# Another order of the same steps: gate logits of the first two spans loaded first, W2 behind the first keys, W1 last of the weights

## The chip, the cores and the metric

The kernel runs on one core of a Trainium2 chip. The metric is the device time in microseconds (us) from start to end of one execution. The kernel before takes 141.34 us, the median of three runs (141.2 to 141.57).

## What is computed

A gated linear recurrence (32 independent sequences of 768 steps, head dimension 48) gives a matrix of 3072 tokens x 384, and that goes through a maxout layer:

```
f = 1 / (1 + exp(-f_logit))
for t in range(768):
    state = f[t][:, None] * state + outer(k[t], v[t])      # 48 x 48 per batch (4) and head (8)
    y[t] = q[t] @ state
x = y of all heads side by side                            # 3072 x 384
out = maximum(x @ w1, x @ w2) @ w_out                      # w1, w2: 384 x 1024, w_out: 1024 x 384
```

All inputs and the output are float32 in HBM; the kernel casts to bf16 for TensorE.

## The kernel before, in words

The tokens are cut into 12 spans of 256: span s has batch s % 4 and window s // 4, so spans 0 to 3 start with an empty state and every later span continues the one four before it. Each span goes through two parts.

- Recurrence, in two halves of 64 token pairs. Loads `Lf`, `Lk`, `Lq`, `Lv` (line 122, 384 KB each) bring the gate logits, keys, queries and values of a span into one of 27 slots of SBUF; the number behind the @ is the slot, and a load into a used slot waits until its last reader is done. On ScalarE (ACT), `E`, `F` and `G` make exp and log of the gate (lines 211, 215, 219). `e` (222) adds the logs of a token pair, the matmuls of `C` (226, 229) sum them up along time, and `X` and `Z` (236, 241) take the exponentials of the sums. `i`, `j`, `K`, `Q` (245, 249, 256, 259) scale the keys and queries, and `V` (a copy, 111) casts the values. TensorE (PE) transposes keys (`t`) and queries (`u`; lines 272 for spans 0 and 1, 279 for the others), `U` copies the transposes to SBUF, `A` (302) makes the scores, `m` (308) masks them, `S` and `y` (323) multiply state and values into the output of the span, `D` (366) makes the addition to the state, and `n`, `N` (383 to 388) bring the state up to date. `z` is a tiny copy that keeps `y` behind the first half of `S`.
- Maxout. Since max(a, b) = b + relu(a - b), the kernel uses wd = w1 - w2 and m2 = w2 @ w_out. `Y` (111) copies the transposed span out of PSUM, `d` (405) multiplies it with wd, `r` (414 on ACT, 416 on VectorE, DVE) is the relu, `o` and `p` (427) multiply with w_out and add x @ m2, `b` (111) copies the result out of PSUM, and `O` (440) stores it.
- The weights are prepared once, in the opening. `Wb0` to `Wb2` (138, 512 KB each) load the rows of W2, which `wc` casts, `wt` (449) transposes and `wx` copies; `Wo0` to `Wo3` (142, 384 KB each) load W_out, and `wo` casts it; `wm0` to `wm3` (464) sum up m2, one quarter for each quarter of W_out, and `wn` copies it out; `Wa0` to `Wa3` (135, 384 KB each) load W1, and `ws` (473) makes wd. They land in slots 0 to 11; the cast and the transposed W2 lie in slots 12 to 15.

The order of everything is written out by hand in one string, `ORDER`: one word for each step, with the span or part, the engine (a ScalarE, v VectorE, p GpSimd (POOL), s SyncE (SP)) and, after the @, a PSUM bank or a slot. `U1.1a@5` is half 1 of `U` of span 1, on ScalarE, from bank 5. A step stands on its engine's queue in the order of its words, and each engine works its queue strictly in that order; across engines only data and buffers (PSUM banks, slots, SBUF buffers) make one wait for another. All loads and stores are on SP's one queue: a load that waits for its slot, or a store that waits for its result, holds up every DMA behind it. The loop that turns words into instructions is

```python
    for word in ORDER.split():
        key, of, e, b = re.fullmatch(r"([A-Za-z]+)([0-9.]+)([avps]?)@?([0-9]*)", word).groups()
        steps[key](*map(int, of.split(".")), e, int(b or 0))
```

Of the kernel before, what the change touches and what calls it, by code (L numbers as in the profile page):

```python
# [17 lines left out]


ORDER = """  # L20
Wb2s Lf1s@8 Lf0s@2 Lq0s@22 g7p Lk1s@24 g6p g4p g2p Wb1s wc2a g5p g0p g3v wt2@5 Lq1s@25 E1 wx2v@5 F1 Lk0s@1
E0 e1p F0 C1@3 Lv1s@20 j0v G1 e0v Z1 C0@7 G0 Wb0s i1v X1 Lv0s@23 Z0 K1v wc1a Q0v t1@1 wt1@3 Wo1s j1v
U1.0a@1 Lf3s@16 Q1v u0@6 X0 Wa3s wx1a@3 i0v u1@5 Wo3s Wo2s U1.1a@5 V1v Wa2s K0v D1@2 Wo0s U0.1a@6 A1.1@0
A1.0@4 Lf2s@20 n1.0 n1.1 t0@7 wc0a m1.0@4 Wa0s V0p wt0@6 U0.0a@7 m1.1@0 D0@4 wo1p S1.0@2 wx0a@6 n0.0
A0.0@0 z1v@2 S0.0@6 n0.1 m0.0@0 z0a@6 A0.1@5 N0.1p y1 g1p m0.1@5 Wa1s E3 Lq3s@13 S1.1@2 S0.1@6 Y1.0a@2 y0
ws3v F3 Lk2s@21 Y0.0v@6 Y1.1a@3 wo3p d1.3@1 wm1@2 wo2a wm3@2 ws2v Lk3s@17 N1.1v d1.2@0 e3v wm2@2 wo0v
r1.1v@0 wm0@2 Lq2s@3 E2 Y0.1v@7 C3@7 F2 d0.3@5 ws0v wn2a@4 wn0a@2 e2v d1.0@0 Lf4s@23 X3 ws1v G3 C2@2
d0.0@6 Z3 wn1v@3 Lf5s@9 X2 d1.1@1 j3v G2 d0.1@7 Q3v r1.0a@0 Lv3s@19 d0.2@4 i2v r0.0a@6 o1.0@0 K2v r0.1a@4
Lv2s@10 i3v Z2 o0.1@7 K3v Lk4s@1 j2v Q2v t2@3 b0.1.0a@7 t3@1 u3@1 b1.0.0a@0 u2@3 E4 U3.2v@1 o0.0@5 U2.0a@3
Lq4s@23 U2.1v@4 Lq5s@24 E5 A3.0@6 Lf7s@17 A3.1@3 F4 V3p m3.0@6 o1.1@0 F5 e4p m3.1@3 G4 V2p b0.0.0a@5 D3@1  # L30
b1.1.0a@0 A2.0@6 e5p n3.0 D2@4 Lk5s@10 m2.0@6 S3.0@0 Lf6s@19 C4@3 z3a@0 i4p S3.1@0 y3 X4 n2.0 Z4 n3.1
S2.0@3 Lv4s@9 Y3.2a@0 A2.1@2 z2v@3 n2.1 S2.1@3 C5@6 m2.1@2 G5 d3.0@0 Z5 Lq9s@26 d3.3@7 X5 j4v j5v y2 Q4p
Lq6s@25 d3.2@6 Y2.2v@3 d3.1@1 r3.1a@6 Lf8s@11 i5v d2.0@5 K4p r3.0v@0 E7 d2.2@3 O0.2s E6 d2.3@4 d2.1@6 F7
K5v Lk6s@12 o3.1@7 F6 Q5p r2.0v@5 r2.1a@3 Lv5s@15 t4@0 V4v t5@4 e6p u5@4 u4@0 U5.2v@4 o2.0@2 U4.2a@0
Lq7s@20 e7p N2.1v j6v Lk7s@3 C6@6 G6 b2.0.0v@2 A4.1@3 E8 D4@0 Lv7s@22 o3.0@2 n4.0 b3.1.0a@7 N3.1v N4.0p
m4.1@3 Z6 X6 Q6p G7 n4.1 S4.0@6 b3.0.0a@2 A5.0@3 A4.0@0 F8 o2.1@2 m4.0@0 Lv6s@25 z4a@6 e8p V5a Lq8s@19
m5.0@3 i6p C7@5 b2.1.0a@2 y4 Z7 K6v X7 S4.1@6 A5.1@2 D5@0 Y4.2a@6 i7p m5.1@2 u6@4 Lf9s@12 t6@4 Lk8s@24
d4.0@6 U6.2a@4 n5.0 O1.2s d4.1@7 N5.0p K7p C8@0 r4.0v@6 d4.2@2 Lv10s@2 G8 d4.3@3 X8 n5.1 Z8 S5.0@6 N4.1p
r4.1a@2 A6.0@4 Lf11s@17 A6.1@0 z5v@6 V6p y5 m6.0@4 N5.1p S5.1@6 D6@2 Lf10s@21 Y5.2a@6 j7v o4.1@4 m6.1@0
V7a Lk10s@15 E9 n6.0 d5.2@0 N6.0p Lk9s@16 F9 b4.1.0v@4 d5.3@1 j9v d5.1@5 j8v r5.1a@0 d5.0@4 Q8p O3.2s  # L40
S6.0@6 r5.0a@4 D7@1 z6v@6 y6 Lq10s@22 Q7v G9 S6.1@6 E11 o4.0@4 e9p n7.0 Y6.2v@6 Lk11s@18 E10 i8v d6.3@7
N7.0v b4.0.0a@4 O2.2s n7.1 F10 d6.2@6 K8v Lv8s@19 d6.1@4 F11 n6.1 e10v C9@0 r6.1a@6 d6.0@3 Lv11s@3 i9p
o5.0@1 r6.0v@3 N7.1p G11 X9 Z9 K9p O4.2s t7@6 t8@2 Lv9s@17 u7@6 u8@2 U7.2a@6 C10@0 o5.1@5 j10v N6.1p
U8.2v@2 e11p b5.0.0a@1 G10 A7.0@6 i11v A7.1@2 b5.1.0a@5 i10p m7.0@6 C11@1 Z10 o6.0@4 O5.2s Z11 Lq11s@0
V10p X10 m7.1@2 X11 K10p V8a S7.0@0 A8.1@6 b6.0.0a@4 A8.0@2 z7v@0 y7 m8.1@6 Q9p S7.1@0 D8@4 o6.1@5 n8.0
Y7.2v@0 V9a V11a m8.0@2 d7.1@1 b6.1.0v@5 d7.0@0 N8.0v O6.2s K11v u9@6 r7.0a@0 t9@6 d7.2@4 U9.2v@6 d7.3@5
S8.0@0 r7.1a@4 D9@3 D10@6 z8v@0 D11@2 n9.0 y8 n10.0 N9.0p S8.1@0 N10.0v A9.1@3 Q10v A9.0@6 Y8.2a@0 o7.0@5
j11v n11.0 Q11p m9.0@6 o7.1@0 b7.0.0a@5 m9.1@3 N11.0p t10@3 b7.1.0v@0 t11@5 u10@3 u11@5 O7.2s U10.2v@3
d8.0@0 U11.1a@6 d8.1@1 U11.0a@5 d8.3@3 d8.2@2 r8.0a@0 S9.0@6 r8.1v@2 A11.1@4 A10.1@0 z9a@6 y9 m10.1@0
S9.1@6 o8.0@3 Y9.2a@6 m11.1@4 A11.0@6 b8.0.0v@3 A10.0@4 S11.0@0 m11.0@6 o8.1@3 m10.0@4 d9.3@7 b8.1.0a@3  # L50
z11v@0 d9.2@6 O8.2s d9.0@2 r9.1a@6 d9.1@3 S10.0@6 r9.0v@2 S11.1@0 y11 z10a@6 y10 Y11.0v@0 S10.1@6 Y11.1v@1
o9.1@5 Y10.2a@6 o9.0@4 b9.1.0v@5 d11.2@1 b9.0.0a@4 d10.0@2 O9.2s r11.4v@1 d10.1@3 d10.2@5 r10.0a@2 d10.3@6
d11.1@3 r10.1a@5 d11.3@2 r11.3v@3 o10.0@7 d11.0@3 b10.0.0v@7 o10.1@0 r11.2v@3 r11.5v@2 o11.0@5 b10.1.0a@0
O10.2s p11.1.1@2 b11.0.0v@5 O11.0s p11.1.0@1 b11.1.2a@2 O11.1.2s b11.1.1a@1 O11.1.1s
"""


# [479 lines left out]
```

## Time and profile before

| quantity | value |
|---|---|
| median of three runs | 141.34 us |
| the profiled execution, its own time | 140.85 us |
| its span, first to last instruction | 138.8 us |
| outside the span | 2.05 us |
| PE busy | 123.0 us (89%) |
| DVE / ACT / POOL busy | 102.6 / 85.0 / 48.7 us |
| moved by DMA | 28.68 MB, mean 207 GB/s |
| share of PE in the chain that ended last | 81% |

The profile is of one execution. Its page gives busy times of each engine, a strip of 40 equal slices of the span (here 3.47 us each), and the chain of work that ended last. The other views are the timeline (instructions in order of time; in brackets the idle time of the engine before one and what ended it), the chain in order of time, and the windows (busy time of each engine in chosen stretches; PEclk is the granted TensorE clock as a share of full speed). PE overlaps one matmul with the next, so two rows of PE can overlap in time, and the steady spacing of a step is shorter than its row.

### The profile page before, as it was taken

How to read it: one execution, taken by the hardware profiler on the slowest of the kernel's cores; microseconds unless marked ns; L12 is line 12 of the kernel's file. 1: busy time of each engine (PE TensorE's matmuls, PEld its weight loads, DVE VectorE, ACT ScalarE, POOL GpSimd, SP SyncE). 2: the span in 40 equal slices, each digit the busy share in tenths (PEclk: the TensorE clock that was granted, in tenths of full speed). 3: DMA queues.
4: the chain of work that ended last, by engine and by line, in shares of the span. 5: the costliest groups of instructions: out<-in, count | busy, mean ns of one | idle time of the engine just before them, and what ended most of it. 6: DMA issues, size and time to landing. Idle time of an engine off the chain costs nothing.

```text
span 138.8 us, 5704 instructions
## 1 busy us (share of the span) xinstructions
PE 123.0 (89%) x2543; PEld 93.7 (68%) x2543; DVE 102.6 (74%) x158; ACT 85.0 (61%) x129; POOL 48.7 (35%) x58
## 2 busy tenths in 40 slices
PE   0225689999999999899899999999999999999991
PEld 0215568868666888566887877676867868778670
DVE  5728799599987979997969599899897592531510
ACT  3797993649869739497798886992533614215020
POOL 7420043200007579729392847793151000000000
PEclk9999975899999999999999999999999999999999
DMA  4999999999999999999999999971202003002033
GB/s 160 281 302 276 316 303 363 322 313 250 269 263 265 264 263 258 290 272 241 225 297 276 243 320 321 321 239 43 113 5 91 32 2 118 5 11 103 0 118 113
DMA packets 55081, 28.68 MB, mean 207 GB/s; under 512 B 50320, under 2 KB 53264, under 8 KB 55056
## 3 DMA queue, kind: packets, MB, share of 16 engines
q1 hardware_dynamic: 55056, 28.32, 77.9%
q8 instruction: 20, 0.33, 1.0%
q14 instruction: 5, 0.04, 0.1%
HBM read 23.59 MB, written 4.72 MB: 204 GB/s over the span
## 4 chain that ended last, share of the span: by engine, by line
PE 81%; SPq 9%; DMA 4%; DVE 2%; issue 1%; POOL 1%; ACT 0%; DVEq 0%
PE banks L427 31%; PE banks L405 23%; PE banks L323 12%; SPq L122 6%; PE banks L302 4%; DMA slots<-in_v_dram 4%; PE banks L279 4%; PE banks L464 3%; SPq L138 3%; PE banks L366 3%; PE banks L226 1%; DVE kp L256 1%; DVE gT L416 1%; POOL vb L111 1%; PE banks L229 1%
## 5 line engine op out<-in xcount | busy, mean ns | idle before, releaser
L427 PE MATMUL banks<-wo,gT 128*128 128x384 bf16 (+1 forms) x200 | 35.2, 320 | 0.0
L405 PE MATMUL banks<-xT,wd 128*128 128x256 bf16 x288 | 34.3, 273 | 0.0
L308 DVE TENSOR_TENSOR at_m<-banks,mask 128x1024 bf16<-128x1024 f32 x24 | 28.5, 1217 | 2.2 <-PE banks L302 2.0
L405 PEld LDWEIGHTS <-wd 128*128 128x128 bf16 x288 | 27.3, 98 | 4.2
L427 PEld LDWEIGHTS <-gT 128*128 128x128 bf16 x200 | 19.3, 98 | 11.8
L414 ACT ACTIVATE gT<-banks 128x1024 bf16<-128x1024 f32 x15 | 15.1, 1023 | 9.5 <-PE banks L405 5.7
L111 ACT COPY ob<-banks 128x384 f32<-128x384 f32 (+1 forms) x17 | 7.7, 462 | 18.7 <-PE banks L427 18.6
L416 DVE TENSOR_SCALAR gT<-banks 128x1024 bf16<-128x1024 f32 (+1 forms) x11 | 11.2, 1027 | 10.1 <-PE banks L405 10.0
L111 ACT COPY trs<-banks 128x1024 bf16<-128x1024 bf16 (+1 forms) x10 | 12.5, 1269 | 7.2 <-PE banks L279 6.6
L427 PE MATMUL banks<-m,xT 128*128 128x384 bf16 (+1 forms) x75 | 15.9, 321 | 0.0
L111 POOL CAST vb<-slots 128x768 bf16<-128x768 f32 x5 | 4.1, 826 | 26.8 <-DMA slots<-in_v_dram 26.8
L259 POOL TENSOR_TENSOR qp<-slots,dec 128x768 bf16<-128x768 f32 x6 | 11.4, 1902 | 5.5 <-DVE slots L249 2.5
L323 PE MATMUL banks<-at_m,vb 64*64 64x128 bf16 x576 | 12.9, 233 | 0.1
L211 ACT ACTIVATE gate<-slots 128x768 f32<-128x768 f32 x12 | 9.9, 843 | 3.5 <-DMA slots<-in_f_logit_dram 3.5
L323 PEld LDWEIGHTS <-vb 64*64 64x64 bf16 x576 | 11.2, 116 | 0.8 <-issue 0.6
L388 POOL TENSOR_TENSOR state<-tmp_s,dec 128x192 bf16<-128x192 f32 x10 | 5.8, 575 | 13.4 <-DVE tmp_s L383 13.4
L222 POOL TENSOR_TENSOR e<-ell 128x384 bf16<-128x384 f32 x8 | 9.3, 1164 | 3.4 <-ACT ell L215 3.0
L215 ACT ACTIVATE ell<-gate 128x768 f32<-128x768 f32 x12 | 9.8, 843 | 0.1
L249 DVE SCALAR_TENSOR_TENSOR slots<-gate,slots 128x384 f32<-128x384 f32 x12 | 7.9, 671 | 2.4 <-DMA slots<-in_q_dram 2.4
L323 PE MATMUL banks<-trs,state 48*64 48x128 bf16 x240 | 9.5, 229 | 0.0
L111 ACT CAST xT<-banks 128x768 bf16<-128x768 f32 (+1 forms) x8 | 5.7, 717 | 5.7 <-PE banks L323 5.5
L111 DVE COPY ob<-banks 128x384 f32<-128x384 f32 x8 | 4.4, 556 | 6.4 <-PE banks L427 3.5
(69 smaller groups left out, 188.1 us busy)
## 6 DMA issues: line engine op xcount, KB each, us to landing
slots<-in_f_logit_dram SPq DMA_DIRECT2D x12, 384.0 KB, 6.1
slots<-in_q_dram SPq DMA_DIRECT2D x12, 384.0 KB, 6.3
slots<-in_k_dram SPq DMA_DIRECT2D x12, 384.0 KB, 6.1
slots<-in_v_dram SPq DMA_DIRECT2D x12, 384.0 KB, 5.9
out_dram<-ob SPq DMA_DIRECT2D x11, 384.0 KB, 3.2
slots<-in_moe_w_dram SPq DMA_DIRECT2D x3, 512.0 KB, 6.1
slots<-in_moe_w_out_dram SPq DMA_DIRECT2D x4, 384.0 KB, 7.2
...
```

What stands on the lines that cost most here:

```text
L111: (nc.scalar.copy if e == "a" else engines[e].tensor_copy)(out, in_)
L122: nc.sync.dma_start(out=slots[:, slot, :].rearrange("p (h x) -> p h x", h=H), in_=src)
L211: nc.scalar.activation(flat(gate[s]), flat(loaded[s]["f"]), AF.Exp, bias=0.0, scale=-1.0)
L215: nc.scalar.activation(flat(ell[s]), flat(gate[s]), AF.Ln, bias=1.0, scale=1.0)
L222: engines[e].tensor_add(pad("e", s)[:, :, 0:D], ell[s][:, :, 0, :], ell[s][:, :, 1, :])
L259: engines[e].tensor_mul(pad("qp", s)[:, :, :, 0:D], by_parity(loaded[s]["q"]), both(dec[s][:, 0:HD].rearrange("p (h d) -> p h d", h=H)))
L308: nc.vector.tensor_mul(at[s][:, jj].rearrange("p r j a t -> p (r j) (a t)"), banks[:, b:b + 2, :].rearrange("p r (j x) -> p (r j) x", j=2) ...
L323: nc.tensor.matmul(out=ys[s][h][c * DP:(c + 1) * DP, blk // 2, :], lhsT=lhs[:, at_col + off:at_col + off + DP], rhs=rhs, start=(s, h, c) n ...
L405: nc.tensor.matmul(out=ps[:, f, :], lhsT=wd[:, fp, kt, f * C:(f + 1) * C], rhs=xT[g][:, kt, :], start=(kt == 0), stop=(kt == KT - 1))
L414: nc.scalar.activation(dst, src, AF.Relu)
L416: nc.vector.tensor_relu(dst, src)
L427: nc.tensor.matmul(out=ps, lhsT=lhs, rhs=rhs[:, out_cols], start=(i == 0), stop=(i == len(terms) - 1))
```

## The change

Only the string `ORDER` changes. Every step is still done once, with the same shapes, and PE has as many matmuls as before; the words stand in another order, and many have another bank, slot or engine. In the opening, in words:

- SP starts with the gate logits of spans 1 and 0, then queries of 0 and keys of 1; the W2 blocks 2 and 1 come behind these. Then queries 1, keys 0, values 1, W2 block 0, and before the values of span 0 now the gate logits of span 3. All four parts of W_out follow (with the gate logits of span 2 between them), and the four parts of W1 are the last of the weights.
- PE starts with `C1` and not with a transpose of W2. `S1.0`, `A0.0` and `A0.1` stand ahead of `D0`, and `C3` goes in between `S0.0` and `S0.1`. After `y0` come `wm3`, `wm1`, `C2`, `wm2` and only then the first `d`; before, a `d` came first and the four `wm` stood in two pairs with a `d` between them.
- Later, `K5` and `i5` move from DVE to POOL and `Q5` from POOL to DVE, `r2.1` and `r3.1` move from ACT to DVE and `r3.0` to ACT. The first store `O0.2` stands ahead of the loads from `Lf7` on. About seventy steps in all change their engine, most of them between DVE and ACT or DVE and POOL.

The diff, cut to the lines on which the prediction rests:

```diff
-Wb2s Lf1s@8 Lf0s@2 Lq0s@22 g7p Lk1s@24 g6p g4p g2p Wb1s wc2a g5p g0p g3v wt2@5 Lq1s@25 E1 wx2v@5 F1 Lk0s@1
...
-d0.0@6 Z3 wn1v@3 Lf5s@9 X2 d1.1@1 j3v G2 d0.1@7 Q3v r1.0a@0 Lv3s@19 d0.2@4 i2v r0.0a@6 o1.0@0 K2v r0.1a@4
...
+Lf1s@11 Lf0s@3 Lq0s@14 Lk1s@10 g0p Wb2s Wb1s E1 Lq1s@19 F1 Lk0s@9 E0 e1p F0 Lv1s@3 C1@1 G1 e0v Z1 Wb0s g1v
...
+Y1.0a@4 y0 F2 wm3@3 Y0.1v@7 e2p Lk3s@23 n0.1 wo1a N0.1v g3p Z3 wm1@3 ws3v G2 wo0a C2@0 wm2@3 Y0.0a@6 G3
...
```

What this makes of three queues. First SP, the queue of all DMAs, from block 0 of W2 to the last part of W1; the names are slots of SBUF and the input that is loaded, in_moe_w_dram with 128x1024 is a block of W2 and with 128x3x256 a part of W1. Before:

```order
L138 DMA slots<-in_moe_w_dram 128x1024
L122 DMA slots<-in_v_dram 128x8x96
L142 DMA slots<-in_moe_w_out_dram 128x2x384
L122 DMA slots<-in_f_logit_dram 128x8x96
L135 DMA slots<-in_moe_w_dram 128x3x256
L142 DMA slots<-in_moe_w_out_dram 128x2x384 x2
L135 DMA slots<-in_moe_w_dram 128x3x256
L142 DMA slots<-in_moe_w_out_dram 128x2x384
L122 DMA slots<-in_f_logit_dram 128x8x96
L135 DMA slots<-in_moe_w_dram 128x3x256 x2
```

and now, from the same block of W2 on:

```order
L138 DMA slots<-in_moe_w_dram 128x1024
L122 DMA slots<-in_f_logit_dram 128x8x96
L122 DMA slots<-in_v_dram 128x8x96
L142 DMA slots<-in_moe_w_out_dram 128x2x384
L122 DMA slots<-in_f_logit_dram 128x8x96
L142 DMA slots<-in_moe_w_out_dram 128x2x384 x3
L135 DMA slots<-in_moe_w_dram 128x3x256 x4
```

The values of span 0 have one load more ahead of them; part 1 of W_out, which was first of its four, is now the last, five loads behind those values; and W1 stands behind all of W_out.

Second ACT, around the casts of W_out (wo) in the opening, from the gate of span 3 on (gate, ell and one are the results of E, F and G; look is z, xT is Y, inv and dec are X and Z, m2 is wn). Before:

```order
L211 ACTIVATE gate_1_162<-slots_71 128x768
L111 CAST xT_1_498<-banks_67 128x6x64
L215 ACTIVATE ell_1_165<-gate_1_162 128x768
L111 CAST xT_1_498<-banks_67 128x6x64
L111 CAST wo_137<-slots_71 128x768
L211 ACTIVATE gate_0_168<-slots_71 128x768
L215 ACTIVATE ell_0_171<-gate_0_168 128x768
L111 CAST m2_138<-banks_67 128x384 x2
```

and now:

```order
L211 ACTIVATE gate_1_146<-slots_71 128x768
L111 COPY look_381<-banks_67 128x1
L215 ACTIVATE ell_1_149<-gate_1_146 128x768
L211 ACTIVATE gate_0_152<-slots_71 128x768
L111 CAST xT_1_493<-banks_67 128x6x64
L236 ACTIVATE inv_1_176<-banks_67 128x384
L111 CAST xT_1_493<-banks_67 128x6x64
L215 ACTIVATE ell_0_155<-gate_0_152 128x768
L111 CAST wo_137<-slots_71 128x768
L241 ACTIVATE dec_3_571<-banks_67 128x392
L219 ACTIVATE one_0_179<-ell_0_155 128x384
L111 CAST wo_137<-slots_71 128x768
```

E and F of span 2 (gate_0, ell_0) and X of span 3 have come ahead of the cast of W_out part 1, which is the first wo here, and two casts of W_out are on ACT where one was.

Third DVE, from the queries of spans 4 and 5 (two j, line 249) to the transposes of span 5 (kp and qp are the scaled keys and queries, gT is the relu r, xT is Y). Before:

```order
L249 SCALAR_TENSOR_TENSOR slots_71<-gate_1_162,slots_71 128x8x48
L111 CAST xT_2_1116<-banks_67 128x2x6x64
L245 TENSOR_TENSOR slots_71<-slots_71,one_1_180 128x8x48
L416 TENSOR_SCALAR gT_1_591<-banks_67 128x1024
L256 TENSOR_TENSOR kp2_102<-slots_71,inv_1_194 128x16x48
L416 TENSOR_SCALAR gT_0_668<-banks_67 128x1024
L111 CAST vb0_110<-slots_71 128x16x48
```

and now:

```order
L249 SCALAR_TENSOR_TENSOR slots_71<-gate_0_152,slots_71 128x8x48
L259 TENSOR_TENSOR qp2_108<-slots_71,dec_0_183 128x16x48
L383 TENSOR_TENSOR tmp_s_2_1119<-banks_67,state4_122 128x192
L416 TENSOR_SCALAR gT_1_623<-banks_67 128x1024
L416 TENSOR_SCALAR gT_0_668<-banks_67 128x1024 x2
L111 COPY trs_1_205<-banks_67 128x2x16x64
```

`i5` and `K5` (lines 245 and 256) are gone from between the relus of spans 3 and 2, `Q5` (259) has come ahead of them, and both relus of span 2 stand on DVE.

More of the change, by code (lines that the diff above doesn't have):

```diff
@@ L31 @@
[L31 to L50, printed above, removed]
@@ new lines @@
+D11@6 D9@2 z8v@0 D10@7 y8 n9.0 n10.0 n11.0 S8.1@0 A9.1@2 N11.0p A9.0@6 Y8.2a@0 m9.1@2 o7.0@4 Q10p m9.0@6
+o7.1@2 N10.0p b7.0.0v@4 N9.0v t10@6 b7.1.0a@2 t11@3 u10@6 O7.2s u11@3 d8.1@1 U11.0v@3 U11.1a@4 d8.0@0
+U10.2v@6 d8.2@2 r8.0a@0 d8.3@3 S9.0@6 r8.1a@2 A11.1@4 A10.1@0 z9v@6 y9 m10.1@0 S9.1@6 o8.0@2 Y9.2a@6
+m11.1@4 A10.0@0 A11.0@6 S11.0@4 m10.0@0 o8.1@3 z11a@4 b8.0.0v@2 m11.0@6 d9.1@1 b8.1.0a@3 d9.2@2 O8.2s
+d9.0@0 d9.3@3 S11.1@4 r9.1v@2 S10.0@6 y11 z10a@6 r9.0a@0 y10 Y11.1v@5 S10.1@6 Y11.0v@4 o9.1@2 Y10.2v@6
@@ L55 @@
+o9.0@6 b9.1.0a@2 d10.3@1 b9.0.0v@6 d11.3@5 O9.2s d10.2@0 r11.5v@5 d10.1@6 r10.1a@0 d10.0@5 d11.2@4
+r10.0a@5 d11.0@3 r11.4v@4 o10.0@7 r11.2a@3 d11.1@0 b10.0.0a@7 o10.1@5 r11.3v@0 p11.1.1@1 b10.1.0a@5 O10.2s
+o11.0@6 b11.1.2a@1 O11.1.2s p11.1.0@5 b11.0.0a@6 O11.0s b11.1.1a@5 O11.1.1s
 """
```

36 lines of the change are left out of this document (24 added, 12 removed).

## The prediction

> **What bounds the kernel now.** I read the page first: busy times, then the strip of 40 slices.
>
> ```profile
> PE 123.0 (89%) x2543; PEld 93.7 (68%) x2543; DVE 102.6 (74%) x158; ACT 85.0 (61%) x129; POOL 48.7 (35%) x58
> ...
> PE   0225689999999999899899999999999999999991
> ...
> PEclk9999975899999999999999999999999999999999
> DMA  4999999999999999999999999971202003002033
> ```
>
> PE is short of full only in the first six slices and is full from then on; the DMA engines are full for the first 26 slices, about 90 us. So the loads decide when PE can begin, and PE decides the rest. The windows give it in numbers:
>
> ```profile
> 0.00:20.00 20.00, 8.24 (x135) 6.83 (x139) 13.51 (x38) 15.19 (x20) 6.20 (x19) 0.97 1.06 272
> 20.00:25.80 5.80, 5.67 (x185) 5.32 (x185) 4.58 (x7) 3.28 (x7) 2.60 (x4) 0.51 1.09 351
> 25.80:35.45 9.65, 9.65 (x83) 7.39 (x83) 8.82 (x14) 6.38 (x12) 0.00 (x0) 1.00 1.14 283
> 35.45:67.90 32.45, 31.48 (x736) 22.56 (x735) 28.87 (x37) 24.57 (x41) 18.23 (x15) 1.00 1.15 265
> 67.90:135.90 68.00, 67.95 (x1423) 51.64 (x1415) 46.84 (x66) 35.29 (x51) 21.63 (x20) 1.00 0.48 141
> ```
>
> Behind 67.90 PE has 0.05 us of idle in 68 us; whatever comes late there is carried to the end one to one, and a new order can win nothing by PE's records. Between 35.45 and 67.90 it idles 0.97 us. In the opening it idles much, and from 20 to 25.8 it is busy at half clock (0.51). So the change can win in two places, before 35.45 (the start of `o1.0`) and in the waits up to 67.90, and lose in both. I use two marks: the start of `o1.0`, and the first transposes of span 6 at 67.88. All PE steps ahead of `o1.0` are the same in both orders, so its start measures the opening.
>
> **The opening, part by part.** The rows on which it rests, from the timeline, and below it four from the chain in order of time:
>
> ```profile
> 13.27 0.56 DVE L249 SCALAR_TENSOR_TENSOR slots<-gate,slots 128x384 f32<-128x384 f32 x1 [0.30 <-DMA slots<-in_q_dram]
> 16.23 0.56 DVE L111 CAST vb<-slots 128x768 bf16<-128x768 f32 x1 [0.89 <-DMA slots<-in_v_dram]
> 19.07 0.82 POOL L111 CAST vb<-slots 128x768 bf16<-128x768 f32 x1 [10.78 <-DMA slots<-in_v_dram]
> 19.94 0.63 PE L366 MATMUL banks<-vb,kp 64*64 64x48 bf16 x32 [0.29 <-POOL vb L111]
> 21.84 1.95 PE L323 MATMUL banks<-at_m,vb 64*64 64x128 bf16 x44
> ...
> 25.72 0.83 ACT L111 CAST wo<-slots 128x768 bf16<-128x768 f32 x1
> 25.78 0.83 PE L405 MATMUL banks<-xT,wd 128*128 128x256 bf16 x6
> 29.44 0.84 ACT L211 ACTIVATE gate<-slots 128x768 f32<-128x768 f32 x1 [2.89 <-DMA slots<-in_f_logit_dram]
> ```
>
> ```profile
> 26.61 1.95 PE banks L464 x12
> 32.73 0.16 PE banks L226
> 32.90 0.08 PE banks L229 x4
> 32.98 2.64 PE banks L405 x24
> ```
>
> The first loads. Taking one 512 KB block of W2 from the head brings the first gate logits sooner, but after two blocks and the same four loads the queue has moved the same bytes, so `Lq1` still lands at 13.27, `Lv1` at 16.23 (two loads, 1.48 us each) and W2 block 0 behind it. What E1, C1 and the first transposes win, 1.3 us at most, ends in the wait for `Lq1` (`j1`, `Q1`, `u1`, `A1`). I cost it at nothing.
>
> The values of span 0 have one load more ahead: 19.07 + 1.48 = 20.5 us, `V0` 0.82, so `D0` starts at 21.4 instead of 19.94. The cover is that `S1.0`, `A0.0` and `A0.1` now stand ahead of it. `D0` at half clock then holds `y1` until 21.4 + 0.45 = 21.85, and before it started at 21.84. Cost nothing; `S0.0` and `C3` are still to do, 0.5 us at half clock, so `y0` ends at 26.4 instead of 25.8, and `wm3` at 27.4.
>
> W_out. From 19.07 to 29.44 eight loads of 384 KB landed, 1.30 us each. Part 1 is now the fifth behind the values of span 0: 20.5 + 5 x 1.30 = 27.0 us, its cast on ACT (0.83) behind E2 and F2 is done at 27.7 to 27.9. `wm1` waits for that, and behind `wm1` on PE stand all the others: three `wm` (1.95 / 2 each), `C2` (0.24) and eight `d` (2.64 / 4 each): 2.93 + 0.24 + 5.28 = 8.45 us. `o1.0` starts at 27.7 + 8.45 = 36.15 us against 35.45: **+0.7 us**. Before, PE had a `d` at 25.78 to fill this place. The parts of W1 follow 1.30 us apart from 28.3 to 32.2 and each has its `d` more than a microsecond later, so they add nothing; if W1 were 1 us later still, the `d` of parts 0 and 1 would wait.
>
> Bounds: were PE alone to decide (27.4 + 8.45), it is +0.4; with the five loads at 1.48 each, part 1 lands at 27.9, and it is +1.8 with its cast and hand-overs of 0.1.
>
> The half clock is the other unknown, since the opening gives PE other gaps:
>
> ```profile
> 16.00:18.00 2.00, 1.16 (x69) 1.02 (x69) 1.69 (x3) 2.00 (x3) 0.00 (x0) 1.00 1.14 299
> 18.00:20.00 2.00, 1.36 (x19) 1.04 (x20) 1.94 (x3) 1.86 (x3) 0.82 (x1) 0.70 1.16 315
> ...
> 65.86 0.89 PE L323 MATMUL banks<-at_m,vb 64*64 64x128 bf16 x48
> ```
>
> With PE 1.16 of 2 us busy the clock fell to a half within the next 2 us, though PE was idle for only 0.84 us of them, and `y` takes over twice its later 0.89. I expect the same pattern, since PE is as sparse at 15 to 21 us. [...]
>
> **The stretch up to 67.90.** The waits there, from the timeline:
>
> ```profile
> 47.85 0.53 ACT L219 ACTIVATE one<-ell 128x384 f32<-128x384 f32 x1
> 49.49 2.00 POOL L259 TENSOR_TENSOR qp<-slots,dec 128x768 bf16<-128x768 f32 x1 [2.51 <-DVE slots L249]
> 49.50 1.10 PE L323 MATMUL banks<-at_m,vb 64*64 64x128 bf16 x48
> 51.45 1.82 POOL L256 TENSOR_TENSOR kp<-slots,inv 128x768 bf16<-128x768 f32 x1
> 51.51 2.17 DVE L245 TENSOR_TENSOR slots<-slots,one 128x384 f32<-128x384 f32 x1
> ...
> 54.74 1.43 DVE L256 TENSOR_TENSOR kp<-slots,inv 128x768 bf16<-128x768 f32 x1
> 56.09 1.21 DVE L416 TENSOR_SCALAR gT<-banks 128x1024 bf16<-128x1024 f32 x1
> 57.36 0.39 PE L279 MATMUL banks<-ident,kp 64*128 64x64 bf16 x15 [0.57 <-DVE gT L416]
> 62.96 0.84 PE L302 MATMUL banks<-trs 48*64 48x128 bf16 x32
> 67.69 0.25 PE L366 MATMUL banks<-vb,kp 64*64 64x48 bf16 x9 [0.37 <-issue]
> ...
> 71.63 0.62 PE L302 MATMUL banks<-trs 48*64 48x128 bf16 x32
> ```
>
> The largest: DVE did `i5` (2.17) and `K5` (1.43) between two relus, so `r2.0` freed its bank late and PE stood 0.57 us. With `i5` and `K5` on POOL this wait goes. What is late next is `K5` on POOL: from 49.49, 2.00 + 1.82 + 1.0 for `i5` (an estimate: half the elements of a `K`, so about half its 1.82) + 1.82 ends at 56.1, and PE's turn for it is near 57; cover 0.9 us. Further `y2` is stretched by 1.10 - 0.89 = 0.21, the `A` of spans 4 and 5 by 0.84 - 0.62 = 0.22, and 0.37 at `D5` has no releaser. Their neighbours are reordered, and a PE that comes 0.7 us later meets results that are 0.7 us older, so I take all four as gone: 0.57 + 0.21 + 0.22 + 0.37 = **-1.4 us**; at least -0.6, at most that.
>
> New waits: `G5` (0.53) now stands on ACT ahead of `Z4`, `X4` and the copy `Y3.2`, for which `A2.1` and `d3.0` on PE wait; between 0 and 0.53, I take **+0.3**. The store `O0.2` in front of `Lf7` holds SP until the copy of `o0.0`, about 3 us later than `Lf7` was issued, but at that time three or four loads of 1.48 are still under way and feed the DMA engines; the wait costs PE nothing while `E7`, at 52, has its gate logits. The other moves between DVE, ACT and POOL exchange rows of the same length (a `b` or a `Y` on either side) on engines that are 61 to 74% busy: nothing.
>
> Sum: +0.7 - 1.4 + 0.3 = -0.4 us. Against the profiled execution (span 138.8, outside it 2.05, time 140.85) this is 140.45; the median lies 0.49 higher, so 141.34 - 0.4 = **140.9 us**.
>
> **The rivals.** What a measurement of this kernel can tell from no change is about 0.3%, 0.42 us.
>
> - The forecast, 140.9, within 140.5 and 141.3: chance 0.40, half of it (0.21) faster, 0.19 the same.
> - [...] Chance 0.20, all faster.
> - W_out comes late, the rival on the other side: with the loads at 1.48, `wm1` starts at 28.8, `o1.0` 1.8 later than before; less 1.4, and 0.3 on top, is +0.7, 142.0. It decides from the point where part 1 lands after 27.7, since the opening then loses more than the waits behind it give back. For it: input loads did take 1.48. Against: the eight loads that included W_out averaged 1.30. Chance 0.22, slower.
> - DVE and POOL hold each other up: `i5` took 2.17 on DVE beside `K4` on POOL, though `K5` with twice its elements took 1.43, and it ended 0.4 behind `K4`. Now `Q5` on DVE meets `Q4`, `K4`, `i5` and `K5` on POOL; if it waits for one of them, `r3.1` behind it on DVE frees its banks late and `d2.1` on PE stands: by half a `K4` (0.9) if the two meet at any offset, so 141.8. [...] Chance 0.18: faster 0.02, the same 0.09, slower 0.07.
>
> Together: faster 0.21 + 0.20 + 0.02 = 0.43, the same 0.19 + 0.09 = 0.28, slower 0.22 + 0.07 = 0.29. The range from 139.8 (the open clock with 0.4 to spare) to 142.2 (late W_out with 0.2 on top) leaves out what lies beyond: a second half-clock window, or an opening that wins.
>
> **What would show it right or wrong.** In the profile after: `D0` near 21.4, `wm1` near 27.7 with the cast of W_out as its releaser, `o1.0` near 36.15 (the opening is wrong by what it differs); no wait of PE for a relu on DVE before the transposes of spans 4 and 5; the first transposes of span 6 near 67.5 and PE full from there on. I am wrong if `o1.0` starts before 35.45, if PE waits behind 68 us for a load or a bank, or if the clock is half at another time than 19 to 25.5.

## The result: slower by 1.4%, and the profile after

The changed kernel takes 144.13 us (median of four runs), the kernel before, run beside it, 141.45 us. The ratio is 1.0143, 95% interval 1.0095 to 1.0191. The forecast was 140.9 us, range 139.8 to 142.2. Runs over 1.5% above the fastest of their kernel, here one of 147.1 us, are left out of every ratio and of the medians given with the experiments, and where a profile is of such a run (the kernel once more, the late loads, the kernel before with spare products), stops, packets and marks are read from it but no totals.

The profiled execution took 144.07 us, span 142.3, against 138.8 before. That is 3.2 us more than the profiled execution before took, while the ratio stands for 2.0 us: what follows takes apart this one pair of executions. First its page: busy times of PE, the strips, and two rows of the table of DMA queues (packets, MB, share of 16 engines).

```profile
PE 122.3 (86%) x2543; PEld 92.2 (65%) x2543; DVE 93.2 (66%) x154; ACT 86.7 (61%) x131; POOL 53.4 (38%) x60
...
PE   0038759999999959999979999999999999999990
...
PEclk9999995699999999999999999999999999999999
DMA  4999999999999999996899999996203002011032
...
q8 instruction: 20, 0.33, 1.0%
q14 instruction: 6, 0.05, 0.1%
```

PE does the same matmuls in 0.7 us less busy time. The half clock lasts 6.8 us as before, but lies at 20.9 to 27.7 us and not at 18.8 to 25.6. PE's strip has two dents that it did not have, a 5 in slice 15 (from 50 us) and a 7 in slice 21 (from 71 us). The same stretches as in the prediction, with the marks of this run (`o1.0` at 36.73, first transposes of span 6 at 69.13, end of the last matmul at 138.51):

```profile
26.43:36.73 10.30, 10.19 (x81) 7.43 (x78) 8.82 (x14) 6.92 (x13) 1.43 (x2) 0.94 1.10 284
36.73:69.13 32.40, 30.55 (x734) 21.96 (x732) 25.13 (x35) 24.34 (x40) 20.87 (x18) 1.00 1.03 241
69.13:138.51 69.38, 68.15 (x1424) 51.85 (x1415) 41.43 (x62) 37.58 (x54) 22.42 (x21) 1.00 0.50 146
```

Against before: up to `o1.0` 36.73 - 35.45 = +1.28; to span 6 32.40 - 32.45 = -0.05; to the last matmul 69.38 - 68.00 = +1.38; from there to the end of the span 3.79 - 2.90 = +0.89. Together +3.5, the whole difference of the spans. The rows behind it, from the timeline:

```profile
21.16 0.63 PE L366 MATMUL banks<-vb,kp 64*64 64x48 bf16 x32 [1.08 <-POOL vb L111]
...
22.85 0.75 PE L323 MATMUL banks<-at_m,vb 64*64 64x128 bf16 x19 [0.24 <-issue]
...
27.42 0.83 ACT L111 CAST wo<-slots 128x768 bf16<-128x768 f32 x1 [0.53 <-issue]
...
36.73 0.49 PE L427 MATMUL banks<-m,xT 128*128 128x384 bf16 x2
...
52.46 0.65 PE L323 MATMUL banks<-at_m,vb 64*64 64x128 bf16 x31 [1.72 <-issue]
...
59.09 0.64 PE L279 MATMUL banks<-ident,qp 64*128 64x64 bf16 x32
59.57 0.63 PE L279 MATMUL banks<-ident,kp 64*128 64x64 bf16 x32
...
74.92 0.81 PE L323 MATMUL banks<-at_m,vb 64*64 64x128 bf16 x44 [1.14 <-issue]
```

The transposes of spans 4 and 5 (59.09, 59.57) wait for no relu any more. But PE now stands 1.72 us in the middle of `y2` and 1.14 us in the middle of `y5`, with no releaser ("issue": the profile shows nothing that it waited for). I call such idle time a stop. (The rows give a stop's idle time; the expectations below count from the start of one matmul to the start of the next, which makes these two 1.94 and 1.35 us.) Counting tells what kind of place that is. If windows of the whole run are cut inside the stops, the numbers of matmuls and weight loads (the first two in brackets) between the cuts are:

```profile
0.00:22.60 22.60, 9.78 (x223) 7.87 (x224) 16.36 (x43) 15.30 (x21) 7.54 (x19) 0.96 1.08 272
22.60:51.50 28.90, 27.66 (x513) 20.23 (x512) 23.57 (x36) 20.01 (x35) 9.54 (x11) 0.91 1.14 285
51.50:74.30 22.80, 21.32 (x512) 16.15 (x512) 16.44 (x24) 18.02 (x26) 18.24 (x17) 1.00 0.93 234
```

447 stand ahead of the stop in `y1`; the 1025 behind them count a matmul that runs across the cut at 22.6 us once more, so it is 1024, and then 1024 again. One matmul whose weights are loaded ahead of the stop starts only behind it. Counted with it, the stops sit at 448, 1472 and 2496, each 448 and a multiple of 256. In the kernel before the short stops sit at such places as well:

```profile
0.00:22.60 22.60, 10.84 (x223) 9.27 (x224) 16.05 (x43) 16.76 (x22) 7.97 (x22) 0.92 1.07 280
22.60:67.40 44.80, 43.99 (x897) 32.65 (x896) 39.23 (x52) 32.31 (x56) 19.05 (x16) 0.97 1.15 276
```

447 and then 1793, counted in the same way, make 448 and 2240, and 2240 is the 0.37 at `D5`. Queue q8 moves 20 packets in the span, 0.33 MB, 16384 B each: one for each 256 of PE's 2543 matmuls and 2543 weight loads. (q1 carries the loads and stores, 28.32 MB.) The packet for the instructions from the 1473rd on lies here (the DMA view of 46.66 to 49.80 us, and behind the dots of 49.80 to 50.79):

```profile
q1 hardware_dynamic: 1413, 0.87, 102.5%
...
q1 hardware_dynamic: 765, 0.29, 111.6%
q8 instruction: 1, 0.02, 6.2%
```

PE enters the block ahead (its 1217th instruction) at 46.66; for 3.14 us there is no packet on q8 while q1 is full, then one from 49.80 to 50.79, and PE goes on at 52.46. So my theory, called instruction blocks: a block of 256 PE instructions is fetched once the block ahead of it is begun; the packet stands behind the loads in the DMA engines, and PE stops at the end of a block if it has used up its 256 instructions before the new ones are there. How late a packet is, I count from the first instruction of the block ahead: 3.14 us here, and from 1.6 us early to 4.0 us late over the 20 packets of this run. The rival, own wait: `y2` and `y5` wait for something that they themselves use.

The tail, by the DMA view of the last 4 us of after (138.0 to 142.3) and of before (135.0 to 138.8):

```profile
GB/s 0 0 0 0 0 0 0 0 0 286 371 329 429 314 100 0 200 321 348 65 0 0 0 0 21 21 14 0 0 0 0 0 0 0 0 0 0 0 0 0
...
q14 instruction: 1, 0.01, 1.0%
...
out_dram<-ob SPq DMA_DIRECT2D x1, 96.0 KB, 2.5
```

```profile
GB/s 0 32 32 0 0 0 162 388 323 404 356 307 130 121 315 340 227 33 0 0 0 0 146 331 323 203 33 0 0 0 0 0 0 0 0 0 0 0 0 0
...
out_dram<-ob SPq DMA_DIRECT2D x2, 96.0 KB, 1.6
```

The last store lands 2.5 us after its issue, not 1.6. Nearly all of it is through by 140.2 us, and its last trickle of 21 GB/s follows half a microsecond later. In the same window q14 has one instruction packet (8192 B); before has none there. The trace of before has 184 ScalarE instructions, waits included, and that of after 194. Theory: ScalarE has now begun one more block of instructions, and its packet sits in front of a part of the last store. Rival: the new order of the last stores.

### The profile page after: what moved, and what is told of

The parts are those of the page before. It is cut to its first block, busy times and chain, and to the rows that moved or that the text cites. A ratio compares the mean times of both kernels' runs of the same rounds, so it can differ in the third digit from the quotient of the medians.

```text
span 142.3 us, 5723 instructions
## 1 busy us (share of the span) xinstructions
PE 122.3 (86%) x2543; PEld 92.2 (65%) x2543; DVE 93.2 (66%) x154; ACT 86.7 (61%) x131; POOL 53.4 (38%) x60
## 3 DMA queue, kind: packets, MB, share of 16 engines
q1 hardware_dynamic: 55056, 28.32, 75.3%
## 4 chain that ended last, share of the span: by engine, by line
PE 74%; DMA 9%; DVE 5%; SPq 4%; issue 4%; ACT 2%; DVEq 0%
PE banks L427 31%; PE banks L405 23%; PE banks L323 8%; DMA slots<-in_q_dram 5%; DMA slots<-in_moe_w_out_dram 4%; PE banks L279 4%; PE banks L302 3%; SPq L122 2%; PE banks L464 2%; PE banks L366 2%; DVE at_m L308 2%; SPq L138 1%; PE banks L226 1%; DVE qp L259 1%; DVE kp L256 1%
## 5 line engine op out<-in xcount | busy, mean ns | idle before, releaser
L405 PEld LDWEIGHTS <-wd 128*128 128x128 bf16 x288 | 27.7, 98 | 4.3
L414 ACT ACTIVATE gT<-banks 128x1024 bf16<-128x1024 f32 (+1 forms) x17 | 16.7, 996 | 10.0 <-PE banks L405 10.0
L222 POOL TENSOR_TENSOR e<-ell 128x384 bf16<-128x384 f32 x10 | 10.4, 1038 | 24.0 <-ACT ell L215 24.0
L416 DVE TENSOR_SCALAR gT<-banks 128x1024 bf16<-128x1024 f32 (+1 forms) x9 | 9.3, 1046 | 13.5 <-PE banks L405 12.7
L245 POOL TENSOR_TENSOR slots<-slots,one 128x384 f32<-128x384 f32 x8 | 8.0, 1004 | 16.2 <-DMA slots<-in_k_dram 13.4
L111 ACT CAST xT<-banks 128x768 bf16<-128x768 f32 (+1 forms) x11 | 7.8, 709 | 8.0 <-PE banks L323 8.0
L111 ACT COPY trs<-banks 128x1024 bf16<-128x1024 bf16 (+1 forms) x8 | 10.6, 1328 | 3.1 <-PE banks L279 2.9
L256 POOL TENSOR_TENSOR kp<-slots,inv 128x768 bf16<-128x768 f32 x6 | 11.8, 1970 | 0.2
L226 PE MATMUL banks<-e,u_inc 128*128 128x384 bf16 x12 | 4.4, 369 | 7.9 <-POOL e L222 7.2
L111 DVE COPY trs<-banks 128x2048 bf16<-128x2048 bf16 (+1 forms) x8 | 8.0, 1014 | 4.4 <-PE banks L279 4.4
L259 POOL TENSOR_TENSOR qp<-slots,dec 128x768 bf16<-128x768 f32 x5 | 9.7, 1945 | 2.7 <-DVE slots L249 1.9
```

What stands on the lines that cost most here:

```text
L111: (nc.scalar.copy if e == "a" else engines[e].tensor_copy)(out, in_)
L222: engines[e].tensor_add(pad("e", s)[:, :, 0:D], ell[s][:, :, 0, :], ell[s][:, :, 1, :])
L256: engines[e].tensor_mul(pad("kp", s)[:, :, :, 0:D], by_parity(loaded[s]["k"]), both(inv[s]))
L259: engines[e].tensor_mul(pad("qp", s)[:, :, :, 0:D], by_parity(loaded[s]["q"]), both(dec[s][:, 0:HD].rearrange("p (h d) -> p h d", h=H)))
L405: nc.tensor.matmul(out=ps[:, f, :], lhsT=wd[:, fp, kt, f * C:(f + 1) * C], rhs=xT[g][:, kt, :], start=(kt == 0), stop=(kt == KT - 1))
L414: nc.scalar.activation(dst, src, AF.Relu)
```

## The experiments

**Once more.** The changed kernel, unchanged.

> The changed kernel once more, unchanged. Theory (instruction blocks): TensorE's instructions arrive by queue q8 in 20 packets of 16384 B, 256 instructions each; counted by their starts, TensorE stops only at the 449th, 1473rd and 2497th of its matmuls and weight loads, all 449 plus a multiple of 256, so every stop sits at such a place again (y2 about 1.9 us, y5 about 1.35 us), its length following how late the packet starts, and the time is 144.1 us (142 to 144.5). Rival (own wait): y2 and y5 wait for something that they themselves use; the stops sit in y2 and y5 again and the time is the same. This run only shows how far the stops repeat; it does not part the two.

143.31 us (ratio 1.017, 1.0104 to 1.0235). The stops came at the same instructions; that in `y2` was 2.5 us, with the packet 4.2 us late. So the length varies from run to run, the place does not. The strip of the clock differs as well:

```profile
PEclk9999999999999987999999999999999999999999
```

The clock was not half in the opening at all, and `o1.0` came at 36.49 us all the same; it was half from 53.0 to 56.4 us, right behind the stop in `y2`.

**104 instructions more.** In idle time ahead of the first `C`:

```diff
+    def spare(n, b):
+        for _ in range(n):
+            nc.tensor.matmul(out=banks[:, b, 0:2], lhsT=u_inc, rhs=ones2, start=True, stop=True)
+        "x": lambda n, e, b: spare(n, b),
-Lv1s@3 C1@1
+Lv1s@3 x52@7 C1@1
```

> The changed kernel with 52 spare 2-column products (104 TensorE instructions) ahead of the first C, where TensorE stands idle until 7.25 us, so that every later instruction sits 104 places further in its block. Theory (instruction blocks): the stops in the middle of y2 and y5 go, since the block ends are then at old numbers 1369 (in a D or y step near 47.8 us) and 2393 and 2649 (near 72.8 and 74.5 us); between the last two only 1.7 us of TensorE's work lies, so a stop of 1.5 to 4.4 us comes in D6, right behind y5, and there may be shorter ones of up to 1.8 us near 44 to 48 us. Time 141.5 to 146 us. Rival (own wait): the stops stay in the middle of y2 and y5 with 1.9 and 1.35 us, and the time stays within 0.3 us of the changed kernel's, since the spare products lie in idle time.

146.79 us, ratio 1.0392 (1.0338 to 1.0446). The rows (line numbers are 33 lower in this kernel: L290 is `y`, L333 is `D`), and the count up to a cut inside each of three stops:

```profile
27.82 0.55 PE L290 MATMUL banks<-at_m,vb 64*64 64x128 bf16 x20 [1.73 <-issue]
...
49.59 0.24 PE L290 MATMUL banks<-trs,state 48*64 48x128 bf16 x2 [0.56 <-issue]
...
76.91 0.25 PE L333 MATMUL banks<-vb,kp 64*64 64x48 bf16 x2 [2.18 <-issue]
```

```profile
0.00:27.00 27.00, 15.03 (x351) 12.84 (x352) 18.01 (x45) 17.98 (x26) 8.88 (x21) 0.94 1.08 287
27.00:49.30 22.30, 21.21 (x384) 15.39 (x384) 18.16 (x28) 15.85 (x27) 5.95 (x8) 1.00 1.05 256
49.30:76.00 26.70, 24.86 (x640) 18.98 (x640) 21.86 (x29) 21.04 (x32) 21.50 (x18) 1.00 1.05 253
```

Counted as above, the stops sit at 704, 1472 and 2752: again 448 and multiples of 256. `y2` and `y5` run through, and the stop of 2.18 us in `D6` came where it was predicted. The own wait is refuted: 1.5 us of spare work in idle time moved every stop. Not foreseen were the stop of 1.73 us in `y0`, at 27 us, and a time above the expected 146. Part of that is the clock: it was half from 76.87 to 80.28 us, right behind the stop in `D6`, with PE busy throughout, which costs about 1.7 us (an estimate, half of the 3.41 us).

**A whole block more.** The same with `x128@7`, 256 instructions.

> The changed kernel with 128 spare products, 256 TensorE instructions, one whole block, ahead of the first C (52 of them took 1.5 us, so these end at about 5.8 us, before TensorE's first work at 7.3 us). Theory (instruction blocks): every later instruction keeps its place in its block, so the kernel does what the changed one does: stops in the middle of y1, y2 and y5 at the same products, 0.5, 1.9 to 2.7 and 1.3 to 1.6 us, no stop of 2 us in D6 and none in wm1; 144 us. Rival (the spare products themselves cost the 3 to 4 us that 52 of them cost): 147 us or more, with the stops of the kernel with 52 products.

144.65 us, ratio 1.0258 (1.0198 to 1.0318). The stops:

```profile
23.62 0.75 PE L323 MATMUL banks<-at_m,vb 64*64 64x128 bf16 x19 [0.20 <-issue]
...
51.45 1.26 PE L323 MATMUL banks<-at_m,vb 64*64 64x128 bf16 x46
...
74.79 0.81 PE L323 MATMUL banks<-at_m,vb 64*64 64x128 bf16 x44 [0.90 <-issue]
```

Those in `y1` and `y5` are back at the same matmul (x19 and x44 behind them, as in after); that in `y2` shrank to 0.4 us from start to start (a row of 1.26 without a break), its packet being 1.8 us late and not 3.1. None is in `D6`. So 128 spare products leave the stops where they are and 52 move them: position counts, not the work. The time is not quite that of the changed kernel: its ratio is 0.9 to 1.2 points above that of the two measurements of the changed kernel, where 52 products came to 2.2 to 2.5. In the profile the opening is longer (`o1.0` at 37.90): the load `Lk0`, issued at 6.7 us, keeps SP for 2.2 us and not 0.9, and the loads behind it go out 1.4 us later than in the changed kernel. The packet of the added block goes out in that time (6.61 to 7.85 us); whether it held SP up was not tested.

**Loads spread.** PE's order is untouched, only SP's changes:

```diff
-b0.0.0a@5 e5p O0.2s C4@3
+b0.0.0a@5 e5p C4@3
-Q4p Lq6s@9 n2.1
+Q4p Lq6s@9 O0.2s n2.1
-o2.1@0 Lv6s@16 F8
+o2.1@0 Lv6s@5 F8
```

> The changed kernel with the loads spread again: the first output store O0 goes back behind Lq6 on SP's queue, so that Lf7, Lk5 and Lf6 no longer wait for it and then go out in one burst at 46 to 47.5 us; Lv6 goes into slot 5, which is free, and not into slot 16, which E8 frees only at 65.8 us, so that five transfers no longer go out together at 65.9 to 68.9 us. TensorE's order is untouched. Theory (instruction blocks): the packets for the 1473rd and the 2497th instruction start about 1.9 us after they can, as in the kernel before, and not 3.1 and 3.65 us after; the stop in y2 falls from 1.9 to under 0.8 us and that in y5 from 1.35 to under 0.4 us; time 141.4 to 142.6 us. Rival (own wait): both stops stay as they are, 144 us. A third way: the spread loads arrive later or earlier for other steps and new waits of up to 0.5 us come.

142.87 us, ratio 1.0109 (1.0059 to 1.0159), span of the profile 140.5. `y2`, `D5` and `y5` (line numbers 33 lower):

```profile
50.17 0.99 PE L290 MATMUL banks<-at_m,vb 64*64 64x128 bf16 x46
...
67.86 0.25 PE L333 MATMUL banks<-vb,kp 64*64 64x48 bf16 x9 [0.67 <-issue]
...
73.23 0.81 PE L290 MATMUL banks<-at_m,vb 64*64 64x128 bf16 x44 [0.53 <-issue]
```

With the same PE instructions the stop in `y2` is gone (the packet came 1.3 us late, not 3.1), that in `y5` is halved (2.8 for 3.65), and `D5` has one again, as in before. `y5`'s stop was to fall under 0.4 and did not, the time is above the expected range, and its ratio is not clear of the changed kernel's 1.0143. What holds is that the lateness of the packet makes the stop. Nine profiles here have the changed kernel's PE order, and in them the stop in `y2` follows its packet: no idle time where it is 1.3 us late, 0.15 to 0.6 us where it is 1.6 to 2.05 late, 1.45 and 1.7 at 3.1, 2.5 at 4.2. That SP's order makes the lateness is shown for `y5` alone: its packet was 3.4 to 4.0 us late in the six profiles that leave the loads there as in the changed kernel, 2.8 and 3.0 with the loads spread, and 0.9 with loads held back (below). For `y2` it is not shown: the whole block, the twelve copies and the late loads leave SP's order untouched there, and its packet was 1.6 to 2.0 us late in them.

**Both ends.** W_out's parts exchanged (`Wo1s` where `Wo0s` stood, and the other way round), and the last words as in before:

```diff
-p11.1.1@1 b10.1.0a@5 O10.2s o11.0@6 b11.1.2a@1 O11.1.2s p11.1.0@5 b11.0.0a@6 O11.0s b11.1.1a@5 O11.1.1s
+o11.0@6 b10.1.0a@5 O10.2s p11.1.1@1 b11.0.0a@6 O11.0s p11.1.0@5 b11.1.2a@1 O11.1.2s b11.1.1a@5 O11.1.1s
```

> The changed kernel with two edits far apart, each read from its own stretch. First, W_out's part 1 is loaded one place earlier and part 0 one later: wo1a then starts at about 26.9 us behind F2 and not at 27.4 us, wm1 at about 27.75 us and not at 28.30 us, o1.0 about 0.5 us earlier, at 36.2 us. Second, the last five steps stand as in the kernel before (o11.0 ahead of p11.1.1, its store of 192 KB issued 1.5 us ahead of the last one): the stretch from the last matmul's end to the span's end falls from 3.8 to 2.9 us. Together minus 1.4 us if the two stops stay as long as they are: 142.7 us; the stops may change by up to 1 us either way, since the loads shift. Rival: the tail is the last store's own latency whatever lies ahead of it, and stays at 3.8 us.

142.67 us (141.97 to 143.32), ratio 1.0091 (1.0032 to 1.015). The cast of W_out's part 1 and `wm1` (line numbers 33 lower):

```profile
26.63 0.84 ACT L78 CAST wo<-slots 128x768 bf16<-128x768 f32 x1
...
27.52 1.14 PE L431 MATMUL banks<-wo,slots 128*128 128x384 bf16 x6 [0.62 <-ACT wo L78]
```

The cast now stands right behind F2, and `o1.0` starts at 35.94, 0.79 us earlier, and 0.5 to 0.7 us earlier than in the three other profiles of this opening without a half clock (once more, spread loads, twelve copies). So more than half of the opening's loss was W_out's lateness. The 0.49 us that are left were not taken apart; PE still waits 1.3 us ahead of `wm3` and 0.62 ahead of `wm1` for casts of W_out. The tail was 3.5 us and not 2.9; this profile has the q14 packet near its end too. So the order of the last stores is at most about a third of it.

**ScalarE's block ends elsewhere.** Twelve copies of two columns at ScalarE's start in the changed kernel, ten in the kernel before:

```diff
+    def spare_act(n):
+        for _ in range(n):
+            nc.scalar.copy(idle, ones2)
+        "xa": lambda n, e, b: spare_act(n),
-Wb1s E1
+Wb1s xa12 E1
```

> The changed kernel with 12 spare two-column copies on ScalarE at the start, where it waits for the first load until 4.4 us. Theory (a late instruction block of ScalarE): queue q14 brings ScalarE's instructions in packets of 8192 B; the last of them goes out at 139.9 us, among the last store's packets, nine of which come only 0.5 us behind it, and the store lands 2.5 us after its issue and not 1.6; in the kernel before there is no such packet behind 112 us. With 12 instructions more the block ends 12 instructions earlier, near 125 to 131 us, the packet meets no store, and the last store takes 1.6 to 1.8 us: the stretch from its issue to the span's end falls from 3.4 to 2.5 us and the time by 0.8 us, to 143.2 us. Rival (the order of the last stores, or the last store's own latency): the stretch stays at 3.4 us.

> The kernel before with 10 spare copies on ScalarE at the start, so that ScalarE has as many instructions as in the changed kernel. Theory (a late instruction block of ScalarE): a packet of 8192 B now goes out about 1 us behind the last store's issue, that store takes 2.2 to 2.5 us in place of 1.6, and the time grows by 0.6 to 0.9 us, to 142.2 us. Rival (the order of the last stores): nothing changes, 141.5 us.

143.21 us (1.0122, 1.0045 to 1.0199) and 145.66 us (1.0264, 1.0184 to 1.0344). The DMA view of the last microseconds, first the changed kernel with twelve, then the kernel before with ten:

```profile
GB/s 0 0 0 0 0 0 0 0 0 0 0 126 398 361 343 434 343 253 55 0 163 316 352 253 73 0 0 0 0 0 0 0 0 0 0 0 0 0 0 0
...
out_dram<-ob SPq DMA_DIRECT2D x1, 96.0 KB, 1.6
```

```profile
GB/s 25 0 0 0 0 201 376 351 351 289 82 276 339 138 6 0 0 44 276 301 132 0 0 67 0 13 19 13 6 0 0 0 0 0 0 0 0 0 0 0
...
q14 instruction: 1, 0.01, 0.4%
...
out_dram<-ob SPq DMA_DIRECT2D x2, 96.0 KB, 2.1
```

In the changed kernel the packet is gone from the end, the trickle with it, and the store takes 1.6 us with its order untouched. In the kernel before, whose last stores were untouched too, packet and trickle came. From the last matmul to the end it is 2.90 us with twelve copies (3.79 without), and 3.94 in before with ten (2.90 without). The theory of the tail holds in both directions. It holds in all 13 profiles that can be read: the eight with 194 ScalarE instructions have a packet at the end, behind the 191st, and tails of 3.5 to 4.1 us; the two with 184 and the three with 206 have none there, and tails of 2.9. The total of before with ten copies grew by more: I had put them behind a weight cast that this order has ahead of E1, so they delayed E1 to 7.24 us, and with the opening the stop in `y1` grew; that part says nothing on the tail, and the expected 142.2 was a miss.

**More loads where it was quiet.** Ten loads of log-gates that nobody reads, behind `O7.2s` of the changed kernel (`O7.2s Lf0s@1 Lf1s@6 Lf2s@8` and so on).

> The changed kernel with ten more loads of log-gates (384 KB each, into slots that nothing uses any more, read by nobody) behind O7 on SP's queue, where the kernel has no load left: they are under way from 108.8 to about 122 us. TensorE's order and every operand stay as they are. Theory (instruction blocks): the packet for the 4801st instruction, which now starts 0.65 us ahead of the 4545th (118.6 us) with quiet queues, starts 2 to 3 us behind it; the 256 instructions between take 3.3 us, packet and restart take 2.5 to 2.8 us, so TensorE stops in y10 for 1.2 to 2.5 us where it never did; time 145.3 to 146.8 us. Rival (loads do not touch TensorE's instructions): no stop, 144.1 us. O8, put off behind the loads, is not late for anything.

143.28 and 144.02 us, ratio 1.0135 (1.0073 to 1.0196): no slower than the changed kernel. A miss. The packet for the 4801st instruction started 1.0 us late, not 2 to 3, and PE stopped 0.3 us. The one ahead of it did start 2.8 us late, but its block lasts 6.3 us, which hides that. Full queues alone do not make every packet 2 to 3 us late.

**The kernel before with 104 instructions more.** `x52@7` ahead of its first transposes.

> The kernel before with 52 spare products, 104 TensorE instructions, ahead of its first transposes, in idle time. Theory (instruction blocks): its stops (449th, 0.44 us, in y1, and 2241st, 0.56 us, in D5) go from there, and the ends of blocks fall where it works densest: stops of about 2.5 us near 24 to 26 us, about 2 us near 46.5 us and about 3 us in D6 near 72 us, those with numbers 705, 1473 and 2753 counted with the spare ones; together 4 to 9 us more, 145.5 to 150 us. Rival (the kernel before owes its stops to its own steps): 141.4 us as before.

151.58 us, ratio 1.0697 (1.0647 to 1.0748), 10 us for idle work of 1.5, and more than the 150 expected:

```profile
27.28 0.74 PE L323 MATMUL banks<-at_m,vb 64*64 64x128 bf16 x15 [1.10 <-issue]
...
52.99 0.24 PE L323 MATMUL banks<-trs,state 48*64 48x128 bf16 x2 [1.78 <-issue]
...
84.16 0.25 PE L366 MATMUL banks<-vb,kp 64*64 64x48 bf16 x2 [4.21 <-issue]
```

The three stops came at the predicted instructions (705, 1473, 2753) with 1.1, 1.8 and 4.2 us, the last longer than expected; its own, in `y1` and `D5`, are gone. They sum to 7.1 us. In this profile the clock was also half from 82.28 to 89.11 us, beginning within the third stop. The rest of the 10 us was not taken apart.

**All mends, and loads held back.** The spread loads, W_out's part 1 first and the twelve copies; then with SP waiting at chosen slots; then with less of that.

> The changed kernel with the spread loads, with W_out's part 1 ahead of part 0, and with the 12 spare copies on ScalarE. From the kernel with the spread loads (142.3 to 143.2 us): the opening is 0.6 us shorter and the tail 0.8 us, so 141.4 us, with stops at the 449th, 2241st and 2497th TensorE instruction of 0.5 to 0.9 us each left; range 140.3 to 142. If it ends above 142.5 us, one of the gains does not add to the others.

> The kernel with all four mends (spread loads, W_out's part 1 first, 12 spare copies on ScalarE) with SP held back at two places: behind Lv6, Lq8 goes into slot 16, which E8 frees near 63.9 us, and Lf9, with Lv7, Lq9 and Lk8 behind it, goes into slot 26, which K7 frees near 68 us. So few loads are under way when TensorE enters the blocks of the 2241st and of the 2497th instruction (near 62.8 and 66.4 us). Theory (instruction blocks): both packets start under 1.5 us after they can, not 1.8 and 3.0; the stops of 1.1 us in D5 and of 1.0 us in y5 fall under 0.4 us each; from 142.1 us to 140.5 us (139.6 to 141.3), under the kernel before. Rival: the held loads come late for spans 8 to 10 and TensorE waits for their data as long as it gained: 141.8 us or more.

> The kernel with the held loads, held less: Lf9 goes out right behind Lq8 into slot 21, which is free, near 64 us and not at 68.3 us, and Lv7 takes over the wait for K7 in slot 26. In the kernel with the held loads the two stops at the ends of blocks near 66.8 and 71.4 us were gone, and a wait of 0.9 us in y6 at 77.5 us, at no end of a block, and a stop of 0.85 us at 94.1 us had come in their place. If the wait in y6 comes from the late load Lf9, it goes, and the later loads are about 1.4 us earlier, so the stop at 94 us shrinks too: 140.5 us (139.8 to 141.3), about 1 us under the kernel before, with the packet for the 2497th instruction 1.0 to 2.2 us behind its time and no stop over 0.3 us there. If the wait in y6 has another cause it stays: 141.5 us.

141.99 us (ratio 1.0031, 0.9986 to 1.0076), 141.70 (1.0025, 0.9981 to 1.0068) and 141.86 (1.003, 0.9992 to 1.0068): all three level with the kernel before, none better. All mends together do take the loss back, since these intervals end below that of the changed kernel (1.0095 to 1.0191); no single mend is clear of it. In the first the three stops that were left (`y2`, `D5`, `y5`) were 0.5 to 0.9 us long. In the second the packets for the 2241st and 2497th instruction were 0.8 and 0.9 us late, and the stops of `D5` and `y5` are gone as expected, but the held loads gave the gain back, as the rival said:

```profile
66.63 0.44 PE L366 MATMUL banks<-vb,kp 64*64 64x48 bf16 x32
...
71.42 0.86 PE L323 MATMUL banks<-at_m,vb 64*64 64x128 bf16 x46
...
77.72 0.56 DVE L245 TENSOR_TENSOR slots<-slots,one 128x384 f32<-128x384 f32 x1 [1.19 <-DMA slots<-in_k_dram]
78.19 0.15 DVE L111 COPY look<-banks 128x2 f32<-128x2 f32 x1
...
78.39 0.86 PE L323 MATMUL banks<-at_m,vb 64*64 64x128 bf16 x46 [0.73 <-DVE look L111]
```

`y6` waited for `z6` (look), and `z6` stands on DVE behind `i8` (line 245), which waited 1.19 us for the keys of span 8: `Lk8`, which SP had held back behind `Lf9`. With all mends and no holding `i8` does not wait there. So it was a held load, but not `Lf9`, which the third kernel sent earlier while `Lk8` still stood behind a wait for slot 26; its gain of 1 us did not come. (The clock of that kernel's profile was 0.87, and its stops are not read.)

## Why the prediction was wrong, step by step

In short: the sum had terms for data alone. What it left out are the engines' own instructions, which also come by DMA (20 packets on q8 and 6 on q14 in after): PE stopped for them 1.72 us in `y2` and 1.14 us in `y5`, and a packet of ScalarE's put 0.89 us on the end. Beside that one term, W_out, was 0.6 us too small.

- The opening, +0.7: right in mechanism, too small. `D0` was forecast for 21.4 and came at 21.16, `y1` at once behind it, and from `wm1` on PE needed the 8.45 us counted. The mis-sized term is the landing of W_out's part 1, put at 27.0, from five loads at 1.30 us behind the values of span 0. Those landed at 20.23 and part 1 at 27.35, 1.42 us for each. ScalarE was through with F2 at 26.9 and still waited, its cast began at 27.42, and `wm1` followed at 28.3, not 27.7. Measured +1.28, within the bounds of 0.4 to 1.8.
- The half clock at 19 to 25.5 us: not right, and of little weight. It came at 20.9 to 27.7, another time than forecast, which the prediction had named as a sign of being wrong. In three more profiles with the same loads and PE order up to `o1.0` (once more, spread loads, twelve copies) the opening had no half clock. The low end of the range, 139.8 ("the open clock with 0.4 to spare"), and the chance of 0.20 counted on such a clock, with `o1.0` 0.3 us behind before, at 35.75. No run shows that 0.3: in these three `o1.0` started at 36.47 to 36.62, 1.0 to 1.2 us behind before, since PE then stood 1.2 us and waited for the same cast of W_out. The clock was worth 0.1 to 0.3 us.
- The waits up to span 6, -1.4 and +0.3: the waits for data went, and by more than forecast. Without its stop of 1.72 us the stretch is 30.7 us, against 32.1 before without its own of 0.37: -1.4 us for data, where the forecast without that 0.37 comes to -0.7. PE has no other gap over 0.25 us in this stretch, so the +0.3 for new waits did not come. With the loads spread it was 36.62 to 68.04, 31.4 us in all.
- The step that failed is the reading of "0.37 at `D5` has no releaser ... I take all four as gone". It was no wait for a neighbour's result but the end of a block of instructions, and in these runs such ends stayed, whatever data was reordered: all 34 stops over 0.25 us came at one, at whichever step stood there (in `y2` none with its packet 1.3 us late, 1.72 us at 3.1). At `D5` the 0.37 did go, but by luck: its packet was 0.7 us late in this profile and not 1.8, and with the loads spread the stop was back with 0.67. In its place `y2` got 1.72 us, which took back all that the stretch had won.
- "PE full from there on", behind the transposes of span 6, failed by the same mechanism: `y5` +1.14 of the +1.38. I had priced `O0.2` in front of `Lf7` and asked only whether `E7` would have its logits. The wait did what I said, and then the loads held up behind it went out together (`O0.2` at 45.84 us, three loads from 46.25 to 47.52) just as PE entered the block ahead of the 1473rd instruction (46.66); Lv6's wait for slot 16 did the same ahead of the 2497th (five transfers from 65.85 to 68.88, PE at 68.92). Taking both away brought the second packet forward, from 3.4 to 4.0 us late to 2.8; for the first, in `y2`, it is not shown that the burst was the cause.
- The tail had no term and gave +0.89: ten more ScalarE instructions, a block begun, a packet in front of the last store.
- Rivals: DVE and POOL holding each other up was not seen as a wait of PE; W_out late was the nearest, right in place, but 142.0 lacks the stops and the tail.

How a late packet becomes a stop, in numbers: in the 13 profiles that can be read a packet started between 1.9 us before the first matmul or weight load of the block ahead and 4.3 us after it. In before and after it took 0.95 to 1.33 us, once 2.01, and at the five stops of these two PE went on 1.3 to 1.7 us after its end. The ten quickest blocks of the two, full of `y`, `A`, `D` or transposes, used their 256 instructions in 3.3 to 4.6 us.
